# An SSD scan feeding a bilinear layer in split fp32: the down projection's high part as one 512-column product, and two early transfers later in SP's list

## The chip, the cores and the metric

The kernel runs on one core of a Trainium2 chip. The metric is the device time of one execution in microseconds (us); the kernel before has a median of 288.21 us over 3 runs (287.66 to 290.09).

## The reference, cut to what matters

```
y   = attn(x, a, B, C)               # chunked state scan: 4 batches, 8 heads, 768 tokens, 32 values a head
t   = y.transpose(0, 2, 1, 3).reshape(3072, 256)
out = ((t @ w1) * (t @ w2)) @ w3 @ w_out    # 256 -> 1024, 1024 -> 1024, 1024 -> 256, all fp32
```

Since nothing stands between `w3` and `w_out`, the kernel multiplies the two once (a 1024 x 256 matrix) and applies the result as its last layer.

## The kernel before, in words

The 768 tokens of a sequence are cut into 16 chunks of 48, and two chunks of all four batches make a slab of 384 tokens; there are 8 slabs. For each chunk c the scan writes the transposed outputs into `XT` (steps named `c<c>.D0` ... `.l`). A slab s then goes through the up layer: for each of 8 blocks of 128 features, two products `l<s>.<ft>.0` and `.1` (for w1 and w2), each of six matmuls of 384 columns; the gate multiplies the two. The result is kept as a high part, rounded to the short fp32 format that TensorE takes in one pass (fp32r, step `.h` on ScalarE), and a low part, the remainder (step `.l` on GpSimd or VectorE).

The last layer runs for three groups of 128 tokens in each slab (`z<s>.<tk>`, function `down`), 24 groups in all. In a group PE takes, for each of 8 feature blocks, three matmuls of 256 columns into the left half of one PSUM bank: high gate part times high weights, high gate part times low weights, low gate part times high weights. The weights stand in two tiles, `WO[0]` (high, `woh` in the profile) and `WO[1]` (low, `wol`); each matmul brings its own weight load, here of the gate tile, so that the high gate part is loaded twice. `store_a` (step `y<s>.<tk>`) copies the 256 columns from PSUM to a slot of `OB` with ScalarE, and `store_b` (step `y<s>.<tk>d`) sends them to memory. Up products and groups share a ring of three PSUM banks, in the order of the list `ORDER`.

All steps stand in one list written by hand, `PLAN` (line 29 on). Each engine takes its own instructions in the order of this list, so a step that waits holds up what stands behind it on its engine. An entry `+n` is n filler matmuls on zeros of 512 columns in bf16 (`keep_clock`, line 618).

All transfers are issued by SP (`load`, line 157). The ones that matter here, in the order of the list: `w<i>.D` loads the i-th piece of w1 and w2 (two transfers of 256 KB into a slot of `ST`); ScalarE and VectorE turn it into the fp32r weights of the up layer in steps `.A .Y .L .S .H .P`. `k.R1` (line 313) copies a constant table from slot 0 of `RD` to slot 1, which odd chunks from 3 on read. `a.save` (line 336) writes the cumulative sums of the scan to memory (`cd`), from where `c<c>.K` (`load_cum`, line 343: one transfer into `LD`, two into `RD`) reads the decay tables of every chunk from 2 on. `c<c>.X`, `c<c>.T` and `s<s>.N` load inputs of the scan.

Of the kernel before, what the change touches and what calls it, by code (L numbers as in the profile page):

```python
# [29 lines left out]
k.z b.D k.q b.tab a.D c0.T s0.N k.p c0.X w0.D b.clip a.clip b.ln a.ln k.r b.m00:v c1.T a.exp w1.D k.L0 +12 c0.C  # L30
k.I b.m01:v k.X c1.X b.m10:v c0.D0 b.m11:v w2.D k.L1 c0.D1 c0.E0 a.scan k.R0 a.t0:p c1.D0 c0.E1 a.r0:p w0.A:a
k.R1 c0.B0 c1.D1 w3.D c1.E0 c0.B1 c0.M0 c0.M1 c1.B0 c0.M2 c1.E1 c0.M3 w0.Y:v +1 c0.Y c1.B1 a.t1:p w0.L c1.C
a.r1:p c0.Z c0.x0:v c0.x1:a a.save c0.x2:v c0.x3:a c2.X c1.M0 c0.h c1.M1 c1.M2 w1.A:a c1.M3 w0.S +6 c1.Y w1.Y:a
w0.H:v w4.D w0.P:v c2.T c1.h c0.l s1.N w2.A:a c3.X c1.l +5 l0.0.0 w2.Y:a w1.L c2.K w1.S l0.0.1 w1.H:v w5.D
l0.0.a w3.A:a w1.P:v c3.T +1 l0.1.0 c1.Z c3.K w3.Y:a w2.L c1.x0:p l0.1.1 w2.S c1.x1:p l0.1.a c1.x2:p w2.H:v w6.D
w4.A:a c1.x3:p w2.P:v w4.Y:a +2 c2.D0 l0.0.g c2.D1 l0.2.1 w3.L w3.S c2.E0 l0.2.0 c2.E1 c2.B0 w3.H:v w7.D w5.A:a
c2.B1 w3.P:v c2.C l0.2.a l0.1.g w5.Y:a c2.M0 l0.3.0 c2.M1 c2.M2 c2.M3 w4.L l0.3.a c2.Y c4.T w4.S w6.A:a c4.K
c3.D0 c2.Z c3.D1 c3.E0 l0.3.1 o0.D w4.H:v c2.h c3.B0 s2.N w4.P:v c3.E1 c2.x0:p l0.4.1 w6.Y:a c2.l c3.B1 c2.x1:p
l0.2.g c3.C c2.x2:p w5.L w7.A:a c4.X c2.x3:p l0.4.0 c3.M0 c3.M1 w7.Y:a c3.M2 c3.M3 w5.S c3.Y l0.4.a w5.H:v o1.D
c4.D0 w5.P:v c4.D1 c4.E0 l0.5.1 c4.E1 c4.B0 l0.3.g c4.B1 c5.T c3.Z l0.5.0 c5.K l0.4.g c3.x0:p c3.h c3.x1:p c3.l  # L40
l1.0.0 l0.5.a c3.x2:p w6.L c5.X o0.A:a c3.x3:p w6.S l1.0.1 l1.0.a w6.H:v o2.D o0.Y:a w6.P:v c4.C l0.5.g l0.6.1
l1.0.g w7.L l0.6.0 o0.L w7.S l1.1.0 l0.6.a w7.H:v o3.D o1.A:a o0.S w7.P:p l1.1.1 l1.1.a l0.6.g v0.D o1.Y:a
l1.1.g l0.7.0 c4.M0 o1.L l0.7.1 l0.7.a o1.S l1.2.0 v1.D l0.7.g c4.M1 o2.A:a c4.M2 l1.2.1 l1.2.a o2.Y:v l1.3.0
o2.L o2.S l1.3.1 l1.3.a c4.M3 v2.D l1.2.g c4.Y l1.3.g v0.A:a o3.A:v v0.Y:a l1.4.0 o3.Y:v o3.L l1.4.1 v1.A:a v0.L
v0.S v1.Y:a c5.D0 c5.D1 o3.S v0.M v4.D c4.Z v3.D c5.E0 v1.L c4.h c5.B0 v1.S c5.E1 c4.x0:p l1.5.0 c4.l v2.A:a
v5.D c5.B1 c4.x1:p v2.Y:a v1.M c4.x2:p c4.x3:p l1.4.a v2.L c5.C l1.5.a v2.S v2.M v6.D c5.M0 c5.M1 c5.M2 v4.A:a
c5.M3 l1.4.g v4.Y:a c5.Y v3.A:v l1.5.1 v3.Y:v v3.L l1.6.0 v5.A:a v3.S c6.T v5.Y:a v4.L v3.M v7.D v4.S c6.K v5.L
v6.A:a v8.D l1.6.1 v5.S s3.N e0.a v6.Y:v v9.D l1.6.a c6.X e0.b l1.7.1 v6.L v6.S v4.M l1.5.g v10.D c5.Z l1.6.g
c5.x0:p c5.h v5.M c5.x1:p c5.l c5.x2:p v7.A:a c5.x3:p v7.Y:a v6.M v8.A:v v7.L v8.Y:a l1.7.0 v7.S v11.D v7.M
# [649 lines left out]
```

## Time and profile before

| | before |
|---|---|
| median of 3 runs | 288.21 us |
| lowest, highest | 287.66, 290.09 us |
| the profiled execution | 288.77 us |
| its span (first to last instruction) | 287.0 us |
| mean granted TensorE clock | 0.994 |
| DMA, mean over the span | 103 GB/s, 29.46 MB |
| 512-column fillers on PE | 31, mean 468 ns each |
| drain of a group by ScalarE (`ob<-bank`) | 24, mean 372 ns each |

PE is TensorE's matmul stream and PEld its weight loads, which run beside matmuls; DVE is VectorE, ACT is ScalarE, POOL is GpSimd, SP is SyncE. A row of the timeline has start, duration, engine, line, operation, output and input, the count of merged instructions, and in brackets the idle time before it with what ended that. In the windows view each engine has its busy time and, behind an x, its instructions; then come PE's granted clock as a share, the DMA engines' busy share and GB/s. A matmul's listed duration includes its way through the array and overlaps the next one's; PE's pace is therefore read from start to start.

### The profile page before, as it was taken

Reading aid. Unit: us, or ns where it says so; the run is one execution under the profiler, and the core shown is the slowest. Engines: PE = TensorE matmul, PEld = TensorE weight load, DVE = VectorE, ACT = ScalarE, POOL = GpSimd, SP = SyncE. Lnnn points to the kernel's source line nnn. Section 1 sums busy time; section 2 is a strip of 40 time slices with the busy share of each in tenths; the row PEclk is TensorE's granted clock in tenths of the full one; section 3 lists DMA queues with packets and bytes.
Section 4 is the critical chain, followed back from the end, with each engine's and each line's share of the span. In section 5 each row is a group of like instructions: output and inputs, shape, how many; then the busy total and the mean of one; then the engine's idle time right before and its main releaser. Section 6 shows DMA issues by size and latency. Waiting matters only on the chain.

```text
span 287.0 us, 7532 instructions
## 1 busy us (share of the span) xinstructions
PE 278.9 (97%) x3079; PEld 254.0 (89%) x3079; DVE 155.0 (54%) x304; ACT 139.9 (49%) x268; POOL 79.9 (28%) x130
## 2 busy tenths in 40 slices
...
GB/s 162 309 285 237 214 226 190 136 286 218 262 232 202 0 32 48 18 119 90 69 12 94 70 27 59 77 63 61 47 30 57 4 0 2 55 2 0 20 56 37
DMA packets 22817, 29.46 MB, mean 103 GB/s; under 512 B 5530, under 2 KB 13056, under 8 KB 22784
## 3 DMA queue, kind: packets, MB, share of 16 engines
...
q8 instruction: 24, 0.39, 0.6%
...
HBM read 25.54 MB, written 3.29 MB: 100 GB/s over the span
## 4 chain that ended last, share of the span: by engine, by line
PE 90%; POOL 5%; issue 2%; DVE 1%; ACT 1%; POOLq 0%; ACTq 0%
PE bank L155 90%; POOL g L164 2%; POOL rdg L270 1%; POOLq L694 0%; DVE rr L164 0%; POOL xe L307 0%; POOL ldc L270 0%; POOL ls L270 0%; DVE st L161 0%; ACT xe L161 0%; POOL gf L164 0%; ACT xt L161 0%; POOL ut L270 0%; DVE st L488 0%; POOL rr L164 0%
## 5 line engine op out<-in xcount | busy, mean ns | idle before, releaser
L155 PE MATMUL bank<-xt,w 128*128 128x384 f32 x768 | 146.9, 343 | 0.1
L155 PEld LDWEIGHTS bank<-xt,w 128*128 128x128 f32 x768 | 133.7, 189 | 4.2 <-DVE w L164 0.4
L164 POOL TENSOR_TENSOR g<-gf,g 128x384 fp32r<-128x384 f32 x37 | 43.1, 1186 | 99.3 <-PE bank L155 92.3
L155 PE MATMUL bank<-woh,g 128*128 128x256 f32 x384 | 69.4, 281 | 0.4 <-POOL g L164 0.4
L164 DVE TENSOR_TENSOR gf<-gf,bank 128x384 f32<-128x384 f32 x64 | 35.1, 550 | 46.5 <-PE bank L155 44.3
L155 PEld LDWEIGHTS bank<-woh,g 128*128 128x128 f32 x384 | 59.1, 187 | 0.9 <-POOL g L164 0.8
L164 DVE TENSOR_TENSOR g<-gf,g 128x384 fp32r<-128x384 f32 x27 | 31.4, 1203 | 43.3 <-PE bank L155 30.4
L161 ACT COPY gf<-bank 128x384 f32<-128x384 f32 x64 | 31.3, 491 | 46.1 <-PE bank L155 46.0
L155 PE MATMUL bank<-wol,g 128*128 128x256 f32 x192 | 53.6, 279 | 0.0
L155 PEld LDWEIGHTS bank<-wol,g 128*128 128x128 f32 x192 | 36.1, 188 | 0.0
L161 ACT COPY ob<-bank 128x256 f32<-128x256 f32 x24 | 8.9, 372 | 47.0 <-PE bank L155 33.2
L164 POOL TENSOR_TENSOR rr<-bn,rr 128x128 f32<-128x128 f32 x32 | 14.0, 452 | 64.1 <-ACT rr L390 61.4
L161 ACT COPY st<-st 128x512 uint16<-128x512 uint16 x22 | 30.1, 1380 | 1.0 <-DVE mag L478 0.5
L161 ACT CAST g<-gf 128x384 fp32r<-128x384 f32 x64 | 29.4, 514 | 1.8 <-DVE gf L164 1.7
L155 PE MATMUL bank<-wof,mag 128*128 128x256 f32 x128 | 29.6, 380 | 0.0
L155 PEld LDWEIGHTS bank<-wof,mag 128*128 128x128 f32 x128 | 24.1, 190 | 3.1
L164 DVE TENSOR_TENSOR rr<-bank,rr 128x192 f32<-128x192 f32 x64 | 19.5, 350 | 4.5 <-PE bank L155 2.4
L155 PEld LDWEIGHTS bank<-rr,xe 64*32 64x32 f32 x1024 | 15.3, 107 | 7.2 <-issue 5.0
L161 POOL COPY xe<-zz 16x256 f32<-16x256 f32 x28 | 12.7, 454 | 27.6 <-DVE zz L433 17.9
L155 PE MATMUL bank<-rr,xe 64*32 64x64 f32 x1024 | 18.2, 218 | 2.2 <-issue 2.1
L161 ACT CAST xt<-bank 128x384 fp32r<-128x384 f32 x16 | 7.7, 480 | 24.0 <-DVE zz L433 20.6
L390 ACT ACTIVATE rr<-bank 128x384 f32<-128x384 f32 x32 | 14.5, 494 | 9.5 <-PE bank L155 8.0
...
## 6 DMA issues: line engine op xcount, KB each, us to landing
...
```

Of the source, the lines that this page charges most:

```text
L155: return tc.keep_in_program_order(nc.tensor.matmul(*args, **kw))
L161: return ins(nc.scalar.copy(*args) if eng == "a" else {"v": nc.vector, "p": nc.gpsimd}[eng].tensor_copy(*args))
L164: return ins({"v": nc.vector, "p": nc.gpsimd}[eng].tensor_tensor(*args))
L270: ins(nc.gpsimd.affine_select(out=t, in_=t, pattern=pattern, compare_op=op, fill=value, base=base, channel_multiplier=step))
L390: ins(nc.scalar.activation(R[:, hf * G8:(hf + 1) * G8, N:], v["pd", hf], AF.Exp))
```

## The change

`WO` becomes one tile with the two parts side by side, so that high and low weights of one feature block are 512 adjacent columns. For all groups but the last one of the kernel (`LAST`, group 7.2), `down` issues per feature block one matmul of 512 columns (high gate part times high and low weights, into the whole bank) and one of 256 columns (low gate part times high weights, added to the bank's right half). `store_a` then copies the left half with ScalarE as before, and VectorE adds the right half from PSUM to it. Group 7.2 keeps three matmuls of 256 columns and no add. In `PLAN` the entries `k.R1` and `w3.D` move from their place ahead of `c0.B0` and `c1.E0` to directly behind `c2.X`. The rest of the list is the same, broken into lines elsewhere.

```
-k.R1 c0.B0 c1.D1 w3.D c1.E0 c0.B1 ... a.save c0.x2:v c0.x3:a c2.X c1.M0 c0.h
+c0.B0 c1.D1 c1.E0 c0.B1 ... a.save c0.x2:v c0.x3:a c2.X k.R1 w3.D c1.M0 c0.h
...
-    WO = [const.tile([P, FT, DM], F32R, name=f"wo{p}") for p in "hl"]
+    WO = const.tile([P, FT, 2, DM], F32R, name="wo")
...
-        task(f"e{j}.a")(lambda e, fs=fs, pv=pv: copy("a", WO[0][:, fs, :], pv))
-        task(f"e{j}.b")(lambda e, fs=fs, pv=pv: tt("v", WO[1][:, fs, :], pv, WO[0].bitcast(F32)[:, fs, :], ALU.subtract))
+        task(f"e{j}.a")(lambda e, fs=fs, pv=pv: copy("a", WO[:, fs, 0], pv))
+        task(f"e{j}.b")(lambda e, fs=fs, pv=pv: tt("v", WO[:, fs, 1], pv, WO.bitcast(F32)[:, fs, 0], ALU.subtract))
...
-            for k, (l, r) in enumerate(((0, 0), (0, 1), (1, 0))):
-                mm(po, gs[sl, ft][:, l, ts_], WO[r][:, ft, :], start=(ft == 0 and k == 0),
-                   stop=(ft == FT - 1 and k == 2))
+            hi, lo = [gs[sl, ft][:, l, ts_] for l in range(2)]
+            w, end = WO[:, ft].rearrange("p l k -> p (l k)"), ft == FT - 1
+            if (sl, tk) != LAST:
+                mm(po, hi, w, start=(ft == 0), stop=False)
+                mm(po[:, DM:], lo, w[:, :DM], start=False, stop=end)
+                continue
+            mm(po[:, :DM], hi, w[:, :DM], start=(ft == 0), stop=False)
+            mm(po[:, :DM], hi, w[:, DM:], start=False, stop=False)
+            mm(po[:, :DM], lo, w[:, :DM], start=False, stop=end)
...
-        copy("a", ob, po)
+        copy("a", ob, po[:, :DM])
+        if (sl, tk) != LAST:
+            tt("v", ob, ob, po[:, DM:], ALU.add)
...
-        po[sl, tk] = pl_bank[sl, tk][:, :DM]
+        po[sl, tk] = pl_bank[sl, tk]
```

SP's list shows the second part of the change. These are its rows before, from `w2.D` (the first row) to the load of chunk 2's decay tables (`ld` and `rd` from `cd`); `rd<-rd` is `k.R1`, the `st` row behind it `w3.D`, `cd<-gf` is `a.save`, the `xe` row behind that `c2.X`, and the next `st` row `w4.D`:

```order
L158 DMA st<-in_w_dram 128x2x256 x2
L158 DMA rd<-rd 102x768
L158 DMA st<-in_w_dram 128x2x256 x2
L158 DMA cd<-gf 128x576
L158 DMA xe<-in_x_dram 48x512 x2
L158 DMA st<-in_w_dram 128x2x256 x2
L158 DMA bc<-in_Bt_dram 128x640
L158 DMA bn<-in_Bn_dram 128x512
L158 DMA xe<-in_x_dram 48x512 x2
L158 DMA ld<-cd 48x2x48
L158 DMA rd<-cd 3x16x48 x2
```

The same stretch of the changed kernel:

```order
L155 DMA st<-in_w_dram 128x2x256 x2
L155 DMA cd<-gf 128x576
L155 DMA xe<-in_x_dram 48x512 x2
L155 DMA rd<-rd 102x768
L155 DMA st<-in_w_dram 128x2x256 x4
L155 DMA bc<-in_Bt_dram 128x640
L155 DMA bn<-in_Bn_dram 128x512
L155 DMA xe<-in_x_dram 48x512 x2
L155 DMA ld<-cd 48x2x48
L155 DMA rd<-cd 3x16x48 x2
```

`rd<-rd` and `w3.D` stand behind the save and `c2.X`, next to `w4.D` (hence four `st` transfers in a row); from there on the order is the old one.

VectorE's list around the groups of slab 6 and the end, before (`g<-gf,g` are low parts of slab 7's gates, `gf<-gf,bank` gates):

```order
L164 TENSOR_TENSOR gf<-gf,bank_81 128x384
L164 TENSOR_TENSOR gf<-gf,bank_83 128x384
L164 TENSOR_TENSOR gf<-gf,bank_82 128x384
L164 TENSOR_TENSOR g<-gf,g 128x384 x3
L694 UNCONDITIONAL_BRANCH
```

And in the changed kernel, whose banks have other numbers:

```order
L161 TENSOR_TENSOR gf<-gf,bank_80 128x384
L161 TENSOR_TENSOR gf<-gf,bank_82 128x384
L161 TENSOR_TENSOR gf<-gf,bank_81 128x384
L161 TENSOR_TENSOR ob<-ob,bank_82 128x256
L161 TENSOR_TENSOR ob<-ob,bank_80 128x256
L161 TENSOR_TENSOR g<-gf,g 128x384 x3
L161 TENSOR_TENSOR ob<-ob,bank_81 128x256
L161 TENSOR_TENSOR ob<-ob,bank_82 128x256
L161 TENSOR_TENSOR ob<-ob,bank_80 128x256
L701 UNCONDITIONAL_BRANCH
```

Two adds stand ahead of the three low parts, the one of group 6.2 behind them, and the last two are those of groups 7.0 and 7.1.

More of the change, by code (lines that the diff above doesn't have):

```diff
@@ L29 @@
 PLAN = """
[L30 to L49, printed above, removed]
@@ new lines @@
+a.save c0.x2:v c0.x3:a c2.X k.R1 w3.D c1.M0 c0.h c1.M1 c1.M2 w1.A:a c1.M3 w0.S +6 c1.Y w1.Y:a w0.H:v w4.D w0.P:v c2.T
+c1.h c0.l s1.N w2.A:a c3.X c1.l +5 l0.0.0 w2.Y:a w1.L c2.K w1.S l0.0.1 w1.H:v w5.D l0.0.a w3.A:a w1.P:v c3.T +1 l0.1.0
+c1.Z c3.K w3.Y:a w2.L c1.x0:p l0.1.1 w2.S c1.x1:p l0.1.a c1.x2:p w2.H:v w6.D w4.A:a c1.x3:p w2.P:v w4.Y:a +2 c2.D0
+l0.0.g c2.D1 l0.2.1 w3.L w3.S c2.E0 l0.2.0 c2.E1 c2.B0 w3.H:v w7.D w5.A:a c2.B1 w3.P:v c2.C l0.2.a l0.1.g w5.Y:a c2.M0
+l0.3.0 c2.M1 c2.M2 c2.M3 w4.L l0.3.a c2.Y c4.T w4.S w6.A:a c4.K c3.D0 c2.Z c3.D1 c3.E0 l0.3.1 o0.D w4.H:v c2.h c3.B0
@@ new lines @@
+s2.N w4.P:v c3.E1 c2.x0:p l0.4.1 w6.Y:a c2.l c3.B1 c2.x1:p l0.2.g c3.C c2.x2:p w5.L w7.A:a c4.X c2.x3:p l0.4.0 c3.M0
+c3.M1 w7.Y:a c3.M2 c3.M3 w5.S c3.Y l0.4.a w5.H:v o1.D c4.D0 w5.P:v c4.D1 c4.E0 l0.5.1 c4.E1 c4.B0 l0.3.g c4.B1 c5.T
+c3.Z l0.5.0 c5.K l0.4.g c3.x0:p c3.h c3.x1:p c3.l l1.0.0 l0.5.a c3.x2:p w6.L c5.X o0.A:a c3.x3:p w6.S l1.0.1 l1.0.a
+w6.H:v o2.D o0.Y:a w6.P:v c4.C l0.5.g l0.6.1 l1.0.g w7.L l0.6.0 o0.L w7.S l1.1.0 l0.6.a w7.H:v o3.D o1.A:a o0.S w7.P:p
+l1.1.1 l1.1.a l0.6.g v0.D o1.Y:a l1.1.g l0.7.0 c4.M0 o1.L l0.7.1 l0.7.a o1.S l1.2.0 v1.D l0.7.g c4.M1 o2.A:a c4.M2
@@ new lines @@
+l1.2.1 l1.2.a o2.Y:v l1.3.0 o2.L o2.S l1.3.1 l1.3.a c4.M3 v2.D l1.2.g c4.Y l1.3.g v0.A:a o3.A:v v0.Y:a l1.4.0 o3.Y:v
+o3.L l1.4.1 v1.A:a v0.L v0.S v1.Y:a c5.D0 c5.D1 o3.S v0.M v4.D c4.Z v3.D c5.E0 v1.L c4.h c5.B0 v1.S c5.E1 c4.x0:p
+l1.5.0 c4.l v2.A:a v5.D c5.B1 c4.x1:p v2.Y:a v1.M c4.x2:p c4.x3:p l1.4.a v2.L c5.C l1.5.a v2.S v2.M v6.D c5.M0 c5.M1
+c5.M2 v4.A:a c5.M3 l1.4.g v4.Y:a c5.Y v3.A:v l1.5.1 v3.Y:v v3.L l1.6.0 v5.A:a v3.S c6.T v5.Y:a v4.L v3.M v7.D v4.S
+c6.K v5.L v6.A:a v8.D l1.6.1 v5.S s3.N e0.a v6.Y:v v9.D l1.6.a c6.X e0.b l1.7.1 v6.L v6.S v4.M l1.5.g v10.D c5.Z
@@ new lines @@
+l1.6.g c5.x0:p c5.h v5.M c5.x1:p c5.l c5.x2:p v7.A:a c5.x3:p v7.Y:a v6.M v8.A:v v7.L v8.Y:a l1.7.0 v7.S v11.D v7.M
+l1.7.a v8.L v8.S v9.A:a v12.D v9.Y:v l2.0.0 e1.a v9.L e1.b l2.0.1 v10.A:a v9.S v10.Y:a v8.M l1.7.g v13.D l2.0.a c7.T
+v10.L c7.K v10.S v9.M l2.0.g v11.A:a v14.D v11.Y:a v10.M v12.A:v v12.Y:a v11.L v11.S l2.1.0 v15.D v12.L v11.M v12.S
+v13.A:a c7.X v13.Y:a c8.T c6.D0 c6.D1 l2.1.1 c6.E0 v13.L c6.E1 v13.S c6.B0 e2.a c6.B1 c6.C v14.A:a e2.b l2.2.0 v14.Y:a
+c6.M0 c6.M1 c8.K c6.M2 v12.M c6.M3 l2.1.a v14.L v15.A:a v14.S c6.Y l2.1.g v15.Y:a v13.M c6.Z l2.2.a v15.L c6.x0:p c6.h
@@ new lines @@
+v15.S c6.x1:p c6.x2:p c6.l l2.2.1 c6.x3:p v14.M l2.2.g v15.M l2.3.0 e3.a l0.0.h e3.b l2.3.1 l2.3.a l0.0.l:p l0.1.h
+l2.4.0 l2.3.g l0.2.h l0.1.l:p l0.3.h l0.2.l:v c7.D0 l0.3.l:p c7.D1 c7.E0 l2.4.1 c7.E1 l2.4.a c7.B0 c7.C l0.4.h c7.B1
+l2.4.g l0.5.h l0.4.l:p l2.5.0 c7.M0 c7.M1 l0.6.h c7.M2 c7.M3 l0.5.l:p l2.5.1 l2.5.a l0.6.l:v l0.7.h c8.D0 l2.5.g
+l0.7.l:p c8.D1 c8.E0 l2.6.0 s4.N c8.E1 l1.0.h l2.6.1 l2.6.a l1.0.l:p c9.K c7.Y l2.6.g c8.C c7.Z l2.7.0 c7.h c8.B0 c7.l
+c8.B1 l2.7.1 l2.7.a c7.x0:p c8.M0 c8.M1 c7.x1:p c8.M2 z0.0 c7.x2:p l2.7.g c8.X c7.x3:p c8.M3 c9.T z0.1 y0.0 y0.0d z0.2
@@ new lines @@
+y0.1 l1.1.h y0.1d l1.2.h l1.1.l:p c10.K l1.3.h l1.2.l:v l1.4.h l1.3.l:p l1.5.h l1.4.l:v c9.D0 l1.6.h c9.D1 l1.5.l:p
+l1.7.h l1.6.l:v y0.2 l1.7.l:p z1.0 c9.E0 y0.2d c9.E1 c9.B0 c9.X l2.0.h c9.B1 l2.0.l:v c10.T z1.1 y1.0 y1.0d z1.2 y1.1
+l2.1.h y1.1d l2.2.h l2.1.l:p l2.3.h l2.2.l:v l2.4.h l2.3.l:p l2.5.h l2.4.l:v l3.0.0:4 y1.2 l2.5.l:p l2.6.h y1.2d
+l3.0.1:4 l2.6.l:v l3.0.a l2.7.h l3.1.0:4 l3.0.g l2.7.l:p l3.0.h l3.1.1:4 l3.1.a l3.0.l:p l3.2.0:4 l3.1.g l3.2.1:4
+l3.2.a s5.N c8.Y l3.2.g c9.C c8.Z c11.K l3.3.0:4 c8.h c9.M0 c9.M1 c8.x0:a c8.x1:v c8.x2:v l3.3.1:4 l3.3.a c8.x3:v c8.l
@@ new lines @@
+l4.0.l:v l4.2.0:4 l4.1.g l4.2.1:4 l4.2.a s6.N c10.Y l4.2.g c11.C c10.Z c13.K l4.3.0:4 c10.h c11.M0 c11.M1 c10.x0:a
+c10.x1:v c10.x2:v l4.3.1:4 l4.3.a c10.x3:v c10.l l4.4.0:4 l4.3.g c11.M2 c11.M3 l4.4.1:4 l4.4.a c12.X c12.D0 l4.4.g
+c12.D1 c12.E0 l4.5.0:4 c13.T c12.E1 c12.B0 c12.B1 l4.5.1:4 l4.5.a l4.6.0:4 l4.5.g l4.6.1:4 l4.6.a c11.Y l4.6.g c12.C
+c11.Z c14.K l4.7.0:4 c11.h c12.M0 c11.x0:a c11.l l4.7.1:4 l4.7.a c12.M1 c11.x1:v c11.x2:a c11.x3:v z3.0 l4.7.g c12.M2
+c12.M3 c13.X c14.T z3.1 y3.0 y3.0d z3.2 y3.1 l4.1.h y3.1d l4.2.h l4.1.l:p l4.3.h l4.2.l:v l4.4.h l4.3.l:p l4.5.h
@@ new lines @@
+l4.4.l:v l5.0.0:4 y3.2 l4.5.l:p l4.6.h y3.2d l5.0.1:4 l4.6.l:v l5.0.a l4.7.h c13.D0 l5.0.g l4.7.l:p c13.D1 c13.E0
+l5.1.0:4 c13.E1 c13.B0 l5.0.h l5.1.1:4 c13.B1 l5.1.a l5.0.l:v l5.2.0:4 l5.1.g l5.2.1:4 l5.2.a s7.N c12.Y l5.2.g c13.C
+c12.Z c15.K l5.3.0:4 c12.h c13.M0 c13.M1 c12.x0:a c12.x1:v c12.x2:v l5.3.1:4 l5.3.a c12.x3:v c12.l l5.4.0:4 l5.3.g
+c13.M2 c13.M3 l5.4.1:4 l5.4.a c14.X c14.D0 l5.4.g c14.D1 c14.E0 l5.5.0:4 c15.T c14.E1 c14.B0 c14.B1 l5.5.1:4 l5.5.a
+l5.6.0:4 l5.5.g l5.6.1:4 l5.6.a c13.Y l5.6.g c14.C c13.Z l5.7.0:4 c13.h c14.M0 c13.x0:a c13.l l5.7.1:4 l5.7.a c14.M1
@@ new lines @@
+c13.x1:v c13.x2:a c13.x3:v z4.0 l5.7.g c14.M2 c14.M3 c15.X z4.1 y4.0 y4.0d z4.2 y4.1 l5.1.h y4.1d l5.2.h l5.1.l:p
+l5.3.h l5.2.l:v l5.4.h l5.3.l:p l5.5.h l5.4.l:v l6.0.0:4 y4.2 l5.5.l:p l5.6.h y4.2d l6.0.1:4 l5.6.l:v l6.0.a l5.7.h
+c15.D0 l6.0.g l5.7.l:p c15.D1 c15.E0 l6.1.0:4 c15.E1 c15.B0 l6.0.h l6.1.1:4 c15.B1 l6.1.a l6.0.l:v l6.2.0:4 l6.1.g
+l6.2.1:4 l6.2.a c14.Y l6.2.g c15.C c14.Z l6.3.0:4 c14.x0:v c14.h c14.x1:v c14.x2:a c14.x3:v c14.l l6.3.1:4 l6.3.a
+c15.M0 c15.M1 l6.4.0:4 l6.3.g c15.M2 c15.M3 l6.4.1:4 l6.4.a l6.5.0:4 l6.4.g l6.5.1:4 l6.5.a l6.6.0:4 l6.5.g l6.6.1:4
@@ new lines @@
+l6.6.a c15.Y l6.6.g l6.7.0:4 c15.h c15.l l6.7.1:4 l6.7.a z5.0 l6.7.g z5.1 y5.0 y5.0d z5.2 y5.1 l6.1.h y5.1d l6.2.h
+l6.1.l:p l6.3.h l6.2.l:v l6.4.h l6.3.l:p l6.5.h l6.4.l:v l7.0.0:4 y5.2 l6.5.l:p l6.6.h y5.2d l7.0.1:4 l6.6.l:v l7.0.a
+l6.7.h l7.1.0:4 l7.0.g l6.7.l:p l7.0.h l7.1.1:4 l7.1.a l7.0.l:p l7.2.0:4 l7.1.g l7.2.1:4 l7.2.a l7.3.0:4 l7.2.g
+l7.3.1:4 l7.3.a l7.4.0:4 l7.3.g l7.4.1:4 l7.4.a l7.5.0:4 l7.4.g l7.5.1:4 l7.5.a l7.6.0:4 l7.5.g l7.6.1:4 l7.6.a
+l7.7.0:4 l7.6.g l7.7.1:4 l7.7.a z6.0 l7.7.g z6.1 y6.0 y6.0d z6.2 y6.1 l7.1.h y6.1d l7.2.h l7.1.l:p l7.3.h l7.2.l:v
```

52 lines of the change are left out of this document (10 added, 42 removed).

## The prediction

> **What bounds the kernel now.** I read the page's busy shares, then the chain that ended last, then windows over the first 25 us, then the pace of matmuls in the timeline.
>
> ```profile
> PE 278.9 (97%) x3079; PEld 254.0 (89%) x3079; DVE 155.0 (54%) x304; ACT 139.9 (49%) x268; POOL 79.9 (28%) x130
> ...
> PE 90%; POOL 5%; issue 2%; DVE 1%; ACT 1%; POOLq 0%; ACTq 0%
> ```
>
> PE is busy nearly always and is 90% of the chain; VectorE has half of its time free. In order of time the chain reads:
>
> ```profile
> 15.27 2.05 issue
> 17.32 19.34 PE bank L155 x269
> ...
> 122.43 0.60 POOL g L164
> ...
> 126.43 145.59 PE bank L155 x1622
> ...
> 276.88 6.05 PE bank L155 x49
> ```
>
> From 17.32 to 282.9 us PE waits only where a group needs the last low part from POOL (near 126.4 and 276.9). Ahead of it stands a hole of 2.05 us that no instruction ended ("issue"). So two things count: the price of a product in PE's stream, and that hole. Windows around it:
>
> ```profile
> 0.00:15.30 15.30, 13.79 (x222) 6.49 (x222) 9.87 (x28) 8.88 (x16) 10.81 (x36) 1.00 0.83 238
> ...
> 10.90:14.30 3.40, 3.28 (x118) 2.04 (x111) 3.29 (x9) 1.94 (x5) 1.67 (x3) 1.00 1.10 283
> 14.30:17.70 3.40, 1.35 (x51) 0.91 (x50) 2.35 (x5) 1.60 (x3) 0.00 (x0) 1.00 0.96 269
> 17.70:21.10 3.40, 3.40 (x11) 2.44 (x10) 2.88 (x6) 2.33 (x3) 0.00 (x0) 0.50 0.99 313
> 21.10:24.50 3.40, 3.40 (x21) 3.17 (x19) 3.30 (x7) 3.02 (x5) 2.40 (x4) 1.00 0.81 225
> ```
>
> In the window with the hole PE is busy 1.35 of 3.40 us, and in the next one its granted clock is 0.50: the hole costs up to 1.7 us more. The DMA engines are full (0.96 to 1.10) from 10.9 to 21.1.
>
> **Part 1, the products.** In 23 groups, 8 times each, two matmuls of 256 columns become one of 512: the same columns, 184 matmuls and weight loads fewer. The paces:
>
> ```profile
> 249.70 15.59 PE L155 MATMUL bank<-xt,w 128*128 128x384 f32 x89
> 265.13 0.28 PE L155 MATMUL bank<-woh,g 128*128 128x256 f32 x1
> ```
>
> ```profile
> 277.22 0.28 PE L155 MATMUL bank<-wol,g 128*128 128x256 f32 x1
> ...
> 282.52 0.28 PE L155 MATMUL bank<-wol,g 128*128 128x256 f32 x1
> ```
>
> ```profile
> 10.32 0.38 PE L155 MATMUL bank<-zero 128*128 128x512 bf16 x1
> ...
> 12.18 1.47 PE L155 MATMUL bank<-zero 128*128 128x512 bf16 x6
> ```
>
> 384 columns: (265.13 - 249.70) / 89 = 173.4 ns. 256 columns: between the two `wol` rows lie 15 feature blocks of three, (282.52 - 277.22) / 45 = 117.8 ns. No row has 512 columns of 4-byte operands. The straight line through the two gives 55.6 ns per 128 columns and 6.6 ns per matmul, so 229.0 for 512 against 2 x 117.8 = 235.6: 6.6 ns less. From below the gain is nothing, if all is by the column. From above the bf16 fillers bound it: (1.47 - 0.38) / 5 = 218 ns, 17.6 less. I take 6.6, from rows of the same operands: 184 x 6.6 = **1.2 us** (bounds 0 and 3.2). A loss I exclude: a weight load lies beside a matmul as before, and there are fewer.
>
> The Trainium skill (TensorE: Matmul & The Clock Gate, section "Wait — 56ns, not 53.3ns?") has N / 2.4 GHz plus about 2.5 ns at full clock, 215.8 ns for 512 columns. By that rule the gain would be 19.8 ns a pair, an estimate of 3.6 us; the fillers agree with it, the 256- and 384-column rows lie about 9 and 11 ns above it (rival E).
>
> **Part 2, the drain.** 23 adds on VectorE, the right half from PSUM:
>
> ```profile
> L164 DVE TENSOR_TENSOR gf<-gf,bank 128x384 f32<-128x384 f32 x64 | 35.1, 550 | 46.5 <-PE bank L155 44.3 <-ACT gf L161 1.1 <-ACT mag L475 0.7
> L164 DVE TENSOR_TENSOR g<-gf,g 128x384 fp32r<-128x384 f32 x27 | 31.4, 1203 | 43.3 <-PE bank L155 30.4 <-ACT g L161 12.9
> L161 ACT CAST g<-gf 128x384 fp32r<-128x384 f32 x64 | 29.4, 514 | 1.8 <-DVE gf L164 1.7
> ...
> L164 DVE TENSOR_TENSOR rr<-bank,rr 128x192 f32<-128x192 f32 x64 | 19.5, 350 | 4.5 <-PE bank L155 2.4 <-POOL rr L164 1.5
> L161 ACT COPY ob<-bank 128x256 f32<-128x256 f32 x24 | 8.9, 372 | 47.0 <-PE bank L155 33.2 <-issue 13.4 <-ACT g L161 0.4
> ```
>
> Between 350 ns for 192 and 550 for 384 columns, 256 come to 0.42 us: 9.7 us of VectorE's free 132, nothing on the path. The bank is held until the add. Tightest is a slab's third group: ahead of its add VectorE has two low parts (1.20 each), which begin after ScalarE's copy and two casts of the second group's end, 0.37 + 2 x 0.51 = 1.4 us. So the bank comes free about 1.4 + 2.4 + 0.4 = 4.2 us after that end, 1.4 after the third group's own (24 x 118 = 2.8 later). PE first takes two up products, 12 x 173 ns = 2.1 us, into the other banks: 0.7 in hand. Behind an add stand low parts, which wait for ScalarE's casts, and these stand behind the same copies already. Without that cover each add would cost 0.42, 9.7 in all.
>
> What is late next is POOL. Its low parts for the groups at 126.4 and 276.9 start from the end of the group before last, so the shortening of the two groups behind that (2 x 8 x 6.6 = 0.1) goes into the wait, twice: **minus 0.2 us**. The last group keeps its form, so the tail behind PE stays.
>
> **Part 3, the two transfers.** SP's issues, and the first arrival of weights:
>
> ```profile
> 7.59 0.98 SPq L158 DMA_DIRECT2D st<-in_w_dram  x2
> 9.33 0.89 SPq L158 DMA_DIRECT2D rd<-rd  x1
> 10.41 1.30 SPq L158 DMA_DIRECT2D st<-in_w_dram  x2
> ...
> 13.31 0.85 SPq L158 DMA_DIRECT2D xe<-in_x_dram  x2
> 15.09 1.33 SPq L158 DMA_DIRECT2D st<-in_w_dram  x2
> ...
> 18.86 0.42 SPq L158 DMA_DIRECT2D ld<-cd  x1
> ```
>
> ```profile
> 4.09 0.94 SPq L158 DMA_DIRECT2D st<-in_w_dram  x2
> ...
> 9.27 0.67 ACT L475 ACTIVATE mag<-st 128x512 f32<-128x512 f32 x1 [0.47 <-DMA st<-in_w_dram]
> ```
>
> The first weights, issued until 5.03, arrive at 9.27: 4.2 us in the queue. The hole fits a late block of PE's instructions. The page has 24 of these in 0.39 MB; 2 x 3079 instructions over 24 are 257 a block, and PE stands at 444 (222 and 222), which with its semaphore instructions makes two blocks. Blocks over the whole run, in the window 14.7 to 16.1, and PE's progress at 11.2:
>
> ```profile
> q8 instruction: 24, 0.39, 0.6%
> ```
>
> ```profile
> q8 instruction: 1, 0.02, 5.4%
> ```
>
> ```profile
> 0.00:11.20 11.20, 9.84 (x97) 4.05 (x101) 5.92 (x18) 6.09 (x11) 9.25 (x34) 1.00 0.73 222
> ```
>
> The one block from 14.7 to 16.1 is the first; between 11.0 and 14.7 there is none. PE is through with about one block (97 and 101) at 11.2, so a third one asked for then started some 3.5 us later: it seems to have stood behind data. The two moved transfers are 512 + 153 KB of that data; at 283 GB/s, 2.4 us. If all of it stood ahead of the block the hole goes; if one of `w3.D`'s halves came behind it, some 0.6 us stay. I take at most 0.6.
>
> Next is the first up product:
>
> ```profile
> 14.47 1.37 ACT L161 COPY st<-st 128x512 uint16<-128x512 uint16 x1
> ...
> 17.60 0.48 ACT L161 CAST xt<-bank 128x384 fp32r<-128x384 f32 x1 [1.77 <-PE bank L155]
> ...
> 18.11 0.56 DVE L164 TENSOR_TENSOR xt<-bank,xt 128x384 fp32r<-128x384 f32 x1 [1.40 <-ACT xt L161]
> ...
> 21.83 0.68 ACT L475 ACTIVATE mag<-st 128x512 f32<-128x512 f32 x1
> ```
>
> ScalarE is free at 15.84 and could cast 1.77 earlier; with the clock not halved PE would be some 3 us ahead at 22. There chunk 2's decay tables are late: their issues start at 18.86, and 4.2 us of queue end near 23.9, counting the second and third at 19.3 to 20.0. The same bytes stand ahead of them after the change, so they come no sooner. PE reads them here:
>
> ```profile
> 25.06 0.49 PE L155 MATMUL bank<-rd,ld 102*128 102x384 bf16 x2
> ...
> 28.30 0.90 DVE L164 TENSOR_TENSOR rr<-bank,rr 128x192 f32<-128x192 f32 x3 [1.38 <-PE bank L155]
> ```
>
> So most of the 3 us turns into a wait at these tables, and PE goes on at about 24.0 instead of 25.06: **1.0 us** gained. That wait is about as long as the hole was; if it falls so that the clock halves as at 17.70, up to 1.7 us goes, which makes A's own lower side. More than 1.40 + 1.38 = 2.8 is not to be had: so long VectorE waits, at 18.11 behind that cast and at 28.30 for PE, and between them it is nearly full. SP's new place costs `w4.D` about 1.3 us and `w3.D` 4.7: issued by 16.4, landed by 20.6, and read by the 21.83 row, which has 1.2 in hand. `rd<-rd` is read by chunk 3 only. SP, which stands idle 14.16 to 15.09, gets back in step before 18.86; if it does not, the tables move with it (rival D).
>
> The Trainium skill (Runtime: NRT & Kernel Launch, section "Instruction fetch mechanics") gives blocks of 256 instructions, agreeing with 257 here, but room for 2048 on PE and a fetch that is mostly hidden; by that no block would be missing at the 444th and part 3 would give nothing (rival C).
>
> **Sum.** 1.2 - 0.2 + 1.0 = 2.0 us. The profiled execution, 288.77 with a span of 287.0, would become 286.8 with 285.0. It lies 0.56 above the median shown; I take the 2.0 off the median: **286.2 us** (A).
>
> **Rivals.**
>
> B, the tables come in time: then VectorE's 2.8 us are all gained instead of 1.0, 284.4. For it: without `w3.D` ahead the queue is shorter when `a.save` enters. Against: 0.68 MB is only reordered.
>
> C, the hole is not made by the queue, or all of it reappears at the tables: 1.2 - 0.2 = 1.0 remains, 287.2. For it: only the time of the block's start ties it to the data.
>
> D, slower: PE's wait at the tables grows. `w3.D` and `w4.D` now go out in one run of 2.6 us, and if SP issues the tables 1.3 later, they land near 25.3, past the 25.06 at which PE reads them now. That is the point from which it decides: PE would have stood over 3 us, the clock halves for the next window as it did at 17.70 (1.7 us), and 0.25 + 1.7 - 1.0 = 0.95 is lost: 289.2.
>
> E, a 512-column product paces like the fillers: 3.2 instead of 1.2, 284.2. For it: the fillers; against: both rows of 4-byte operands lie above that line.
>
> **Chances.** A 0.47, B 0.14, C 0.20, D 0.09, E 0.10. About 1% is what a measurement of this kernel can tell from no change (285.3 and 291.1). Faster than that: B, E and a little of A, 0.30; slower, beyond D, 0.04; within, 0.66. The range that leaves out 2 in 10 reaches from just under B and E to most of D: 283.9 to 288.9. A alone has 285.2 to 287.9.
>
> **What would show it.** Right: 184 matmuls `wo,g` of 512 columns at 226 to 231 ns from start to start; no hole above 0.6 us near 15.3 and the cast of 17.60 at about 15.9; the first instruction block on its way before 14; a PE wait of over 1 us at the chunk-2 tables, which are read near 24.0; the adds at 0.4 us with no PE wait on a bank; POOL's two waits 0.1 longer. Wrong: a hole of 2 us at 15.3 (part 3), a pace at 218 or 235 (part 1), a half clock after 24 (D), or a PE wait that VectorE's add ends (part 2).

## The result, and the profile after

| | before | after |
|---|---|---|
| median (lowest to highest), 8 runs each | 288.02 us (287.38 to 290.09) | 290.91 us (290.60 to 292.24) |
| ratio, 95% interval | | 1.0105 [1.0077, 1.0133] |
| profiled execution, its span | 288.77, 287.0 us | 290.81, 289.1 us |

The change costs 1.05%, 2.9 us. The forecast was 286.2 us, with a range of 283.9 to 288.9; the time lies above it. In four of the experiments below (`e1_products`, `e4_copy_only`, `e5_w3_only`, `e6_fillers`) one execution took 390 to 695 us; ratios and counts leave it out, and without it no median would move by more than 0.09 us.

The page of the changed kernel, busy shares and the chain's shares:

```profile
PE 279.8 (97%) x2895; PEld 245.2 (85%) x2895; DVE 162.1 (56%) x327; ACT 139.6 (48%) x268; POOL 79.6 (28%) x130
...
PE 91%; DMA 3%; POOL 2%; DVE 1%; issue 1%; POOLq 0%; SPq 0%; ACT 0%; DVEq 0%
```

184 matmuls and weight loads are gone, 23 operations of VectorE have come, and DMA, which had no share of the chain before, has 3%. In order of time the chain shows where (start, length, what), first between 16 and 40 us, then at the end:

```profile
16.45 4.99 DMA st<-in_w_dram
...
21.46 4.93 DMA ld<-cd
...
26.44 13.08 PE bank L152 x236
```

```profile
129.21 147.10 PE bank L152 x1503
...
285.13 0.37 ACT ob L158
```

PE waits for chunk 2's decay tables (`ld<-cd`) until 26.44. From PE's restart after the first of its waits for GpSimd to the last copy, 126.43 to 282.99 before and 129.21 to 285.13 now, it is 156.56 against 155.92 us: the last layer is 0.64 shorter, and all of the loss lies ahead of it. PE in the first 31 us (the timeline; in brackets idle time and what ended it):

```profile
14.81 1.47 PE L152 MATMUL bank<-rr,xe 64*32 64x64 f32 x64
...
17.41 2.38 PE L152 MATMUL bank<-xt,w 128*128 128x384 f32 x12
...
22.25 0.61 PE L152 MATMUL bank<-zero 128*128 128x512 bf16 x2
26.44 0.50 PE L152 MATMUL bank<-rd,ld 102*128 102x384 bf16 x2 [3.58 <-DMA ld<-cd]
26.64 3.60 PE L152 MATMUL bank<-xt,w 128*128 128x384 f32 x12
```

The hole at 15.27 is gone, as forecast: PE goes from the 64 `rr` matmuls on without a stop, and the up products begin at 17.41. But then it stands 3.58 us, where a wait until about 24.0 was forecast, and the 12 products behind that take 3.60 us. The windows of the same stretch (busy time of PE, PEld, DVE, ACT, POOL, then granted clock, DMA share, GB/s):

```profile
14.30:17.70 3.40, 3.40 (x74) 1.90 (x73) 3.33 (x9) 3.32 (x6) 0.00 (x0) 1.00 0.46 121
...
24.50:28.00 3.50, 1.56 (x8) 1.50 (x9) 2.54 (x5) 2.92 (x6) 0.50 (x2) 0.92 0.72 213
28.00:31.40 3.40, 3.40 (x41) 2.80 (x41) 0.20 (x1) 1.77 (x3) 0.28 (x1) 0.58 0.93 251
```

From 14.3 to 17.7 the DMA engines, 0.96 busy before, have work for 0.46 only. And the granted clock, halved before from 17.7 to 21.1, is now halved behind the wait (0.58 over 28.0 to 31.4). SP's issues in the same stretch:

```profile
13.68 0.34 SPq L155 DMA_DIRECT2D cd<-gf  x1
14.13 1.30 SPq L155 DMA_DIRECT2D xe<-in_x_dram  x2
15.52 0.87 SPq L155 DMA_DIRECT2D rd<-rd  x1
16.45 1.94 SPq L155 DMA_DIRECT2D st<-in_w_dram  x4
18.44 0.47 SPq L155 DMA_DIRECT2D bc<-in_Bt_dram  x1
18.95 1.23 SPq L155 DMA_DIRECT2D bn<-in_Bn_dram  x1
20.27 0.84 SPq L155 DMA_DIRECT2D xe<-in_x_dram  x2
21.46 0.33 SPq L155 DMA_DIRECT2D ld<-cd  x1
```

SP issues one transfer after another, and the tables' load goes out at 21.46 instead of 18.86.

The halved clock can be followed in the timed executions too, since each has its mean granted clock. A stretch of 3.4 us at 0.50 makes 0.994 of 287 us. All 8 executions of the changed kernel have 0.994 or less. Of the 110 of the kernel before on the four chips of the experiments, 30 have 0.990 to 0.994 (the profiled one too, 0.994), the other 80 have 0.996 or more. Chip by chip the median of the first kind is 1.1, 1.4, 1.8 and 1.7 us above that of the second (289.0, 289.6, 289.4, 289.4 against 287.9, 288.1, 287.7, 287.7), and there are 3 of 29, 11 of 35, 5 of 29 and 11 of 17 of it, which makes most of the difference between the chips' medians.

### The profile page after: what moved, and what is told of

It reads as the page before. It is cut to its first block, busy times and chain, and to the rows that moved or that the text cites. A ratio compares the mean times of both kernels' runs of the same rounds, so it can differ in the third digit from the quotient of the medians.

```text
span 289.1 us, 7204 instructions
## 1 busy us (share of the span) xinstructions
PE 279.8 (97%) x2895; PEld 245.2 (85%) x2895; DVE 162.1 (56%) x327; ACT 139.6 (48%) x268; POOL 79.6 (28%) x130
## 4 chain that ended last, share of the span: by engine, by line
PE 91%; DMA 3%; POOL 2%; DVE 1%; issue 1%; POOLq 0%; SPq 0%; ACT 0%; DVEq 0%
PE bank L152 91%; DMA st<-in_w_dram 2%; DMA ld<-cd 2%; POOL g L161 2%; POOLq L701 0%; DVE rr L161 0%; DVE mag L491 0%; DVE zz L430 0%; SPq L155 0%; ACT ob L158 0%; DVE xe L158 0%; DVE zero L261 0%; DVE spare L260 0%; DVEq L161 0%; POOLq L161 0%
## 5 line engine op out<-in xcount | busy, mean ns | idle before, releaser
L152 PE MATMUL bank<-wo,g 128*128 128x256 f32 (+1 forms) x392 | 69.0, 335 | 0.4 <-POOL g L161 0.3
L152 PEld LDWEIGHTS bank<-wo,g 128*128 128x128 f32 x392 | 59.5, 188 | 8.9 <-POOL g L161 1.0
L158 ACT COPY gf<-bank 128x384 f32<-128x384 f32 x64 | 31.4, 493 | 47.2 <-PE bank L152 47.2
L161 DVE TENSOR_TENSOR g<-gf,g 128x384 fp32r<-128x384 f32 x27 | 29.7, 1126 | 6.1 <-PE bank L152 3.4
L161 DVE TENSOR_TENSOR ob<-ob,bank 128x256 f32<-128x256 f32 x23 | 9.6, 417 | 34.5 <-ACT ob L158 34.5
L472 ACT ACTIVATE mag<-st 128x512 f32<-128x512 f32 x24 | 16.6, 693 | 4.8 <-DMA st<-in_w_dram 2.6
L158 ACT CAST xt<-bank 128x384 fp32r<-128x384 f32 x16 | 7.8, 486 | 22.2 <-DVE zz L430 20.6
```

Source lines behind the costliest of these rows:

```text
L152: return tc.keep_in_program_order(nc.tensor.matmul(*args, **kw))
L158: return ins(nc.scalar.copy(*args) if eng == "a" else {"v": nc.vector, "p": nc.gpsimd}[eng].tensor_copy(*args))
L161: return ins({"v": nc.vector, "p": nc.gpsimd}[eng].tensor_tensor(*args))
L472: ins(nc.scalar.activation(v["mag"], v["wh"], AF.Copy, scale=2.0 ** -112))
```

## The experiments

Twelve runs on four chips, each beside runs of the kernel before on the same chip (medians there 287.95, 288.64, 287.72 and 289.00 us, in the order of the chips below). Edits are shown as entries of `PLAN`; all but `e2_moves` have the new products. Microseconds are medians, ratios are to the kernel before on the same chip. Each expectation names a theory and a rival by a letter. The first theory, T: the moves cost the time, by way of chunk 2's tables, which come late. Its first rival, P: the products do, with their adds and the bank that these hold.

**The two parts apart.** `e1_products` is the changed kernel with the old order, as below; `e2_moves` is the kernel before with the new order, the same lines the other way round:

```diff
 k.R0 a.t0:p c1.D0 c0.E1 a.r0:p w0.A:a
-c0.B0 c1.D1 c1.E0
+k.R1 c0.B0 c1.D1 w3.D c1.E0
...
-a.save c0.x2:v c0.x3:a c2.X k.R1 w3.D c1.M0
+a.save c0.x2:v c0.x3:a c2.X c1.M0
```

> The change's products and drain with the old order of SP's transfers. Theory T (the loss comes from chunk 2's decay tables, whose first issue waits for the landing of the transfer eight places before it, now w3.D's first half): no loss here, 0.7 to 1.0 us below the kernel before, so 287.0 to 287.4; the tables are read by PE near 25. Rival P (the loss comes from the products or from VectorE's adds holding a bank): about 291 as the changed kernel.

> The old products with the two transfers moved. Theory T: the whole loss and a little more, 3.3 to 3.8 us above the kernel before, so 291.3 to 291.8; PE waits about 3.5 us at chunk 2's tables and its clock is halved for one window after that. Rival P: within 0.5 us of the kernel before.

Measured: 287.31 us, ratio 0.9981 [0.9960, 1.0001], and 292.49 us, 1.0147 [1.0118, 1.0176]. The products lose nothing (a gain of 0.6 us by the medians, which the interval does not tell from none), the moves lose 1.5%. A profile of the products alone follows with `e1_again`. PE in the second, with the same wait at the same place as in the changed kernel:

```profile
26.02 0.73 PE L152 MATMUL bank<-rd,ld 102*128 102x384 bf16 x2 [3.61 <-DMA ld<-cd]
```

So nothing in the products' code is at fault. The loss, 4.5 us, is larger than my theory's 3.3 to 3.8 by 0.7. Three of the six executions have a mean clock of 0.988, as much as two halved stretches would make instead of one; whether that is the 0.7 is not shown.

**The tables earlier in the changed kernel.** `e3_tables_first` puts them ahead of `w4.D`, `e7_tables_mid` behind `c2.T`:

```diff
-w0.H:v w4.D w0.P:v c2.T c1.h c0.l s1.N
+w0.H:v c2.K w4.D w0.P:v c2.T c1.h c0.l s1.N
...
-w1.L c2.K w1.S
+w1.L w1.S
```

```diff
-c0.l s1.N
+c0.l c2.K s1.N
...
-w1.L c2.K w1.S
+w1.L w1.S
```

> The changed kernel with the loads of chunk 2's tables put ahead of w4.D, so that eight places before them stand transfers of w2 and the save, which have landed by 16. Theory T: issued near 17.5 to 18, landed before PE asks at about 22.8, no wait of over 0.5 us there and no halved clock; 284.5 to 286.5. Rival P: 290 to 291, since the wait at the tables would be a symptom only.

> The changed kernel with the loads of chunk 2's tables put ahead of s1.N and c3.X alone, behind w3.D and w4.D. Theory T: their issue waits for c2.X, long landed, instead of w3.D, so they go out near 19 instead of 21.5 and land near 24; the wait at the tables falls from 3.6 to about 1.2 us, the time to 287 to 288.5. Rival Q (the tables are late for the bytes ahead of them alone, whatever the issue waits for): only 0.46 MB less stand ahead, 1.6 us, so the wait falls to 2.0 us with a halved clock, 289 to 290.

Measured: 289.45 us, 1.0041 [1.0019, 1.0064], and 288.63 us, 1.0028 [1.0004, 1.0052]. Of the loss, 1.5 and 0.7 us are left on this chip: the first gives back about half, far less than I expected, the second more, and it lies 0.13 above T's range. PE and ScalarE in the first of them:

```profile
17.10 0.24 PE L152 MATMUL bank<-rr,xe 64*32 64x64 f32 x1 [1.45 <-issue]
...
26.99 0.94 PE L152 MATMUL bank<-bc 32*64 32x96 f32 x28 [0.86 <-ACT rr L387]
```

```profile
24.55 0.68 ACT L472 ACTIVATE mag<-st 128x512 f32<-128x512 f32 x1 [1.62 <-DMA st<-in_w_dram]
...
26.35 0.96 ACT L387 ACTIVATE rr<-bank 128x384 f32<-128x384 f32 x2
```

The wait at the tables is gone, but now ScalarE stands 1.62 us for w4's weights, and chunk 2's exponentials (`rr`), which PE wants, stand behind w4's steps. The weights are late because SP stands from 17.29 to 19.20 ahead of the tables' load into `RD`, until the table copy has landed (why, `e10_both_tables` shows below). In the second kernel PE still waits at the tables, for that load:

```profile
24.59 0.48 PE L152 MATMUL bank<-rd,ld 102*128 102x384 bf16 x2 [1.90 <-DMA rd<-cd]
```

This wait is rival Q's (2.0 us, from the bytes ahead), not T's (1.2). The tables' first load goes out at 20.62, only 0.84 earlier than in the changed kernel, but PE reads them 1.85 earlier: `bn` and the two halves of `c3.X`, 0.45 MB, no longer stand ahead of them.

**One move at a time.** `e4_copy_only` (only `k.R1` moved) and `e5_w3_only` (only `w3.D`), against the old order:

```diff
-k.R1 c0.B0 c1.D1 w3.D c1.E0
+c0.B0 c1.D1 w3.D c1.E0
...
-c2.X c1.M0
+c2.X k.R1 c1.M0
```

```diff
-k.R1 c0.B0 c1.D1 w3.D c1.E0
+k.R1 c0.B0 c1.D1 c1.E0
...
-c2.X c1.M0
+c2.X w3.D c1.M0
```

> The new products, and of the two moves only the table copy (k.R1) behind c2.X; w3's load stays at its old place. Theory T (the loss is the chain of semaphores: chunk 2's table load may only be issued when the transfer eight places before it has landed, and with both moves that is w3's first half): here the transfer eight places before it is half of c2.X, which is in early, so the load is issued before 20 and PE waits at most 1.5 us at the tables: 286.8 to 288.2 us. Rival P (each moved transfer leaves the DMA engines empty for its own length between 14 and 17 us, 313 KB for the copy against 524 KB for w3, so the loss of 3.6 us splits about 3 to 5): 288.4 to 289.2 us.

> The new products, and of the two moves only w3's load behind c2.X; the table copy stays at its old place. T: the transfer eight places before chunk 2's table load is again w3's first half, as in the changed kernel, so PE's wait at the tables is 2.5 to 3.6 us and the halved clock follows: 289.8 to 291.0 us. P: 5 of 8 parts of the loss: 289.2 to 289.8 us, with a shorter wait at the tables.

Measured: 288.01 us, 0.9975 [0.9949, 1.0002], and 289.51 us, 1.0018 [0.9988, 1.0049]. The first lies in T's range; the second is 0.3 below T's, in P's, though its wait is of T's length. The copy alone costs nothing that can be measured; w3's load makes the wait. PE and SP with w3's load alone moved:

```profile
15.92 0.24 PE L152 MATMUL bank<-rr,xe 64*32 64x64 f32 x1 [0.56 <-issue]
...
25.24 0.82 PE L152 MATMUL bank<-rd,ld 102*128 102x384 bf16 x2 [3.03 <-DMA ld<-cd]
```

```profile
18.07 1.51 SPq L155 DMA_DIRECT2D bn<-in_Bn_dram  x1
19.68 0.85 SPq L155 DMA_DIRECT2D xe<-in_x_dram  x2
20.57 0.42 SPq L155 DMA_DIRECT2D ld<-cd  x1
```

The hole shrinks to 0.56 here; with the copy alone moved it stays at 2.00 us, and PE comes to the tables after they have landed. Theory T had a chain of semaphores as the cause: transfers share eight in turn, and one may only be issued when that eight places before it has landed, for the tables w3's first half. The times suit it, the rows do not. Here SP is done with `c3.X` at 20.53 and issues the tables at 20.57, without waiting for anything; in the changed kernel it is done at 21.11 and waits until 21.46 for w3's landing. That chain is worth at most 0.35 us there. What made the load go out late is the run of issues ahead of it. Formed on this: theory S, below. (Why it also landed late is told under the failed step.)

**The price of the halved clock.** `e6_fillers`:

```diff
-w4.Y:a +2 c2.D0
+w4.Y:a +18 c2.D0
```

> The changed kernel with 16 more filler products (512 columns, about 0.21 us each at full clock, 3.4 us in all) ahead of chunk 2's first step, where PE waits 3.6 us for the tables. They keep PE at work through the wait, which itself stays. Theory H (the halved clock after the wait costs 1.5 us of its own): no granted clock of 0.5 after the start, 289.2 to 289.6 us. Rival N (the work behind it waits for late weights anyhow, so the halved clock is hidden, or the fillers themselves hold PE up): 290.3 to 291.3 us.

Measured: 289.41 us, 1.0022 [1.0003, 1.0041]. PE in it:

```profile
21.52 4.06 PE L152 MATMUL bank<-zero 128*128 128x512 bf16 x18
25.91 0.48 PE L152 MATMUL bank<-rd,ld 102*128 102x384 bf16 x2 [0.34 <-DMA rd<-cd]
26.10 2.41 PE L152 MATMUL bank<-xt,w 128*128 128x384 f32 x12
```

The tables come about as late as in the changed kernel, but PE is at work until 25.58. The 12 products behind take 2.41 instead of 3.60 us, the granted clock stays at 1.00, and none of 11 timed executions has a mean clock under 0.997. So the halved clock costs 1.5 us by the medians (290.91 and 289.41), as theory H had it. These come from two chips; the profiles agree: 3.60 - 2.41 us for these 12 products and 0.89 - 0.59 for the 32 small ones behind them, 1.5 in all. The fillers end before the tables come and show no cost.

**The tables earlier in the old order.** `e8_tables_first_old`, the products, in the order of the kernel before `c2.K` alone moved:

```diff
-w0.H:v w4.D w0.P:v
+w0.H:v c2.K w4.D w0.P:v
...
-w1.L c2.K w1.S
+w1.L w1.S
```

> The new products, neither transfer moved, but chunk 2's table loads (c2.K) ahead of w4's weights. Theory T: the queue stays full, the tables come before PE asks, and the wait of about 1 us at 24 us goes: 286.2 to 287.0 us. Rival A (as when the tables were put ahead of w4 in the changed kernel, w4's weights then come late and ScalarE's step on them stands ahead of chunk 2's: the wait only moves to 26 to 34 us): 287.3 to 289.0 us.

Measured: 288.41 us, 0.9979 [0.9955, 1.0004]: as with the products alone, no gain, in the rival's range.

**Theory S: SP's time to issue.** Two kernels take the tables' load out of the run of issues, to directly behind `w4.D`: `e9_w3_tables`, with only w3's load moved, and `e10_both_tables`, the changed kernel; `e1_again` repeats the products alone beside them:

```diff
-w0.H:v w4.D w0.P:v
+w0.H:v w4.D c2.K w0.P:v
...
-w1.L c2.K w1.S
+w1.L w1.S
```

> The new products; w3's load behind c2.X, the table copy at its old place, and chunk 2's table loads (c2.K) pulled up to right behind w4's load, ahead of c2.T, the normalising step's loads and c3.X (five issues of SP). Theory S (the loss is SP's time to issue: 0.4 to 0.5 us a transfer, in order, now behind a.save instead of ahead of it, so all that follows goes out late): the table load is issued at 17.5 to 18.5 instead of 20.6, PE waits at most 0.5 us for it, no halved clock, hole at 15 us under 1 us: 286.6 to 287.6 us. Rival W (the transfers that lose their place, c2.T's and w5's, hold ScalarE up instead): 288.0 to 289.2 us, with PE's waits between 26 and 37 us.

> The changed kernel with chunk 2's table loads (c2.K) right behind w4's load. S: the load is issued at 18 to 18.6 instead of 21.46; its second part has to wait for the table copy, now issued at 15.5, so not before 20; PE waits at most 1 us, the clock is halved in few executions: 287.0 to 288.2 us. W: 288.3 to 289.5 us, with the waits between 26 and 37 us.

> The new products with the old order once more, for an undisturbed profile of them. The 0.65 us by which this kernel was ahead of the one before should stand in the profile between 122 and 285 us, as 23 x 8 products at 7 ns less each (1.3 us at most) less what the last layer then waits for GpSimd near 126 and 277 us: 287.0 to 287.6 us. Rival: the gain sits in the head, and the stretch from 122 to 285 us is as long as before to 0.2 us.

Measured, on one chip: 287.27 us, 0.9978 [0.9959, 0.9996]; 288.34 us, 1.0015 [0.9995, 1.0036]; 287.30 us, 0.9996 [0.9973, 1.0019]. SP and PE in the first:

```profile
14.89 1.96 SPq L155 DMA_DIRECT2D st<-in_w_dram  x4
16.95 0.41 SPq L155 DMA_DIRECT2D ld<-cd  x1
17.40 0.65 SPq L155 DMA_DIRECT2D rd<-cd  x2
```

```profile
14.67 1.36 PE L152 MATMUL bank<-rr,xe 64*32 64x64 f32 x64
...
22.55 0.49 PE L152 MATMUL bank<-rd,ld 102*128 102x384 bf16 x2
```

No hole, no wait at the tables, no halved clock in 12 executions: with w3's load moved and the tables' load ahead of four other issues (S counted five), the move costs nothing, as S had it. Those four carry 0.77 MB, so this run does not tell SP's issues from the bytes ahead. It does not pay either: 287.27 against 287.30 without any move. In the second kernel, with the table copy moved as well:

```profile
18.51 0.47 SPq L155 DMA_DIRECT2D ld<-cd  x1
20.29 0.61 SPq L155 DMA_DIRECT2D rd<-cd  x2
```

```profile
16.64 0.24 PE L152 MATMUL bank<-rr,xe 64*32 64x64 f32 x1 [0.83 <-issue]
...
23.62 0.48 PE L152 MATMUL bank<-rd,ld 102*128 102x384 bf16 x2 [0.69 <-DMA rd<-cd]
```

Between `ld` and `rd` SP stands from 18.98 to 20.29: `k.R1` reads slot 0 of `RD`, chunk 2's tables are written into that slot, and so their load has to wait until the copy, issued at 15.59, has landed. 288.34 lies 0.14 above S's range and just inside W's. The copy's place is worth 1.07 us here (288.34 against 287.27, the same chip).

PE with the products alone:

```profile
17.38 0.24 PE L152 MATMUL bank<-rr,xe 64*32 64x64 f32 x1 [1.50 <-issue]
...
18.45 2.44 PE L152 MATMUL bank<-xt,w 128*128 128x384 f32 x12
...
23.80 2.41 PE L152 MATMUL bank<-xt,w 128*128 128x384 f32 x12
...
27.24 1.31 PE L152 MATMUL bank<-xt,w 128*128 128x384 f32 x6 [0.52 <-DVE gf L161]
```

This execution has the hole, but not the halved clock. Its stretch from PE's restart after GpSimd's first wait to the last copy is 125.49 to 281.50, 156.01 us, against 156.56 before: the products' 0.55 us lie in the last layer, not in the head. The ratio of this chip, 0.9996, does not show so little.

**One more step.** `e11_scalar` is `e9_w3_tables` with one more step of ScalarE moved:

```diff
-w4.A:a c1.x3:p w2.P:v w4.Y:a +2 c2.D0
+w4.A:a c1.x3:p w2.P:v +2 c2.D0
...
-c2.E1 c2.B0
+c2.E1 w4.Y:a c2.B0
```

> The kernel that has w3's load behind c2.X and chunk 2's tables behind w4's load, with one more step moved: ScalarE's copy for w4 (w4.Y, 1.4 us) behind its two exponentials of chunk 2 (c2.E0, c2.E1) instead of ahead of them. Theory A (what that kernel still loses between 24 and 34 us, about 1 us, is ScalarE's order): the exponentials start at about 23.2 instead of 24.3, PE's waits near 25.1 to 26.2 us go: 0.3 to 0.7 us less, a ratio of 0.9955 to 0.9970 to the kernel before. Rival V (VectorE's chain of w2's and w3's steps sets that stretch, as the chain of waits has it): no change, a ratio of 0.997 to 0.999.

Measured: 287.41 us, 0.9950 [0.9924, 0.9976]. The ratio is theory A's, but it comes from the other side: on this chip 11 of 17 executions of the kernel before had the halved clock, and its median was 289.00. Against 287.27 us there is no gain, so this is inconclusive at best and rather V's case. These last two orders, with the tables behind `w4.D` and the copy at its old place, lie below the kernel before on their chips, but not below the products alone (287.30); in 24 timed executions of them the clock was not halved once, against 30 of 110 of the kernel before.

## Why the prediction was wrong

**The failed step** is "the same bytes stand ahead of them after the change, so they come no sooner", from which I took that the tables come no later either, and with it "SP, which stands idle 14.16 to 15.09, gets back in step before 18.86; if it does not, the tables move with it (rival D)". The tables go out at 21.46, and PE reads them at 26.44, where 24.0 was forecast. I counted the bytes ahead of them, but not what the DMA engines have to do meanwhile. Before, `k.R1` and `w3.D` went out while SP had to wait for the scan's sums anyway (9.33 to 12.87), and their bytes kept the engines full through that wait. In the changed kernel SP issues nothing from 8.84 to 13.68, and the engines run dry:

```profile
10.90:14.30 3.40, 3.40 (x104) 2.05 (x105) 2.47 (x8) 1.41 (x4) 2.03 (x4) 1.00 0.81 216
```

That is 216 against 283 GB/s in this window and 121 against 269 in the next one, 0.73 MB less by 17.7 us: about as much as was moved, and 2.6 us at 283 GB/s. From there to 24.5 the engines are 0.90 to 0.95 busy, and the load waits in their queue: by the trace's records of landings it lands at 23.86 us before (the prediction had 23.9) and at 26.39 now, 2.53 later, both times 0.18 us behind the second half of `c3.X`, which went out just ahead of it. With the products alone it lands at 23.55, with the copy alone moved at 23.94, with w3's load alone at 25.19, each time 0.19 to 0.21 behind `c3.X`.

That SP was late by as much, 2.6 us, can be added up too. Behind `c2.X` the three issues of the moved transfers, 15.52 to 17.47, take 1.95 us of a list in which each transfer goes out behind the last. What could absorb that stood in SP's rows before:

```profile
16.97 0.43 SPq L158 DMA_DIRECT2D bn<-in_Bn_dram  x1
18.02 0.79 SPq L158 DMA_DIRECT2D xe<-in_x_dram  x2
```

0.93 us of idle time ahead of `w4.D` and 0.62 here, 1.55 in all: 0.4 too little even by rows. The rest: the save itself 0.81 later (13.68 for 12.87), `c2.X`'s two issues 1.30 us long for 0.85, `bn` 1.23 for 0.43, and the 0.35 of the semaphore; with the 0.4 that makes 2.8. `w4.D`'s own issues, 0.93 for 1.33, take 0.4 back, and small differences add 0.2. Not all of that is the change's: the save also left at 13.47 in an execution with the old order. How much quicker issues behind the save would have helped, with the same bytes, no run shows.

**The hole** went as forecast, and the instruction blocks agree with the reason given. Now the window 13.3 to 14.7 has one, ahead of the 14.7 to 16.1 of before:

```profile
q8 instruction: 1, 0.02, 5.2%
```

The hole is 1.50 to 2.45 us in the profiles of four kernels with w3's load at its old place, and 0 to 0.83 in eight of the nine with it moved (1.45 in the ninth, `e3_tables_first`). In the seven profiles with more than 0.5 us, PE goes on 1.26 to 1.65 us after the last packet of that block, the ninth too (15.69 and 17.10 there, 16.03 and 17.32 before). The Trainium skill (Runtime: NRT & Kernel Launch, section "Instruction fetch mechanics") would have had no block missing here, rival C; these holes speak against it. What the shorter hole gave, PE at its first up product at 17.41 for 18.45 with the products alone, went into the wait at the tables, as forecast, and 2.4 us more.

**The sum of the head**, against the products alone in the old order: 1.04 us ahead at the first up product; at the first one of chunk 2, 26.64 against 23.80, 2.84 behind; then 3.60 against 2.41 us for 12 products, and so on until the clock returns, 1.5 in all by the fillers' run, less 0.6 that the old order loses at 27.24. That is 3.7, and the medians differ by 3.6 (290.91 and 287.31, on two chips).

**Rival D** named place and mechanism, a later issue, PE standing over 3 us, then the halved clock; I gave it 0.09 and 289.2 us. It was mis-sized: the tables were read at 26.44, not 25.3. And the clock was the other half: I priced the halving at "up to 1.7 us", 1.5 measured, but set it down as A's lower side, though the wait that A itself had was to be as long as the hole that had just halved the clock in the profile.

**The products** were mis-sized. The price of a 512-column product was right, that of its neighbour was not. A block of three groups in the changed kernel, and in the one before:

```profile
184.78 8.53 PE L152 MATMUL bank<-wo,g 128*128 128x512 f32 x48
193.16 0.33 PE L152 MATMUL bank<-xt,w 128*128 128x384 f32 x1
```

```profile
182.17 0.28 PE L155 MATMUL bank<-woh,g 128*128 128x256 f32 x1
...
190.65 0.34 PE L155 MATMUL bank<-xt,w 128*128 128x384 f32 x1
```

(193.16 - 184.78) / 24 = 349.2 ns for a product of 512 and one of 256, (190.65 - 182.17) / 24 = 353.3 for three of 256: 4.1 ns saved, not 6.6. By the median from start to start in the trace's records, the 512 columns take 229 ns, as the straight line had it, but the 256 behind them 119 instead of 117.8, and 120 or more in about a third of the records. 184 x 4.1 = 0.75 us, less GpSimd's two waits: 0.64 and 0.55 in the two profiles where 1.2 - 0.2 = 1.0 was forecast. The Trainium skill's rule (TensorE: Matmul & The Clock Gate, section "Wait — 56ns, not 53.3ns?"), 215.8 ns for 512 columns, rival E, is not borne out for these operands.

**The drain** was right:

```profile
L161 DVE TENSOR_TENSOR ob<-ob,bank 128x256 f32<-128x256 f32 x23 | 9.6, 417 | 34.5 <-ACT ob L158 34.5
```

0.42 us each, and among what PE waits for there is no bank that this add holds.

**w3's weights**, which I had landed by 20.6 with 1.2 us in hand, were late as well: ScalarE's step on them begins at 22.22 instead of 21.83, after 2.56 us of waiting. It does not set the end only because PE stands at the tables anyway. And "`rd<-rd` is read by chunk 3 only" was true of what it writes; that it reads a slot which chunk 2's load overwrites showed when that load was pulled up.
